# Reordering the opening of an attention-then-mixer kernel: one load queue, half rows, and a first tile that gets its gain in the product

## The chip, the cores and the metric

The kernel runs on one core of one Trainium2 chip. A core has engines with instruction streams of their own: TensorE (PE, matmuls; PEld is its loading of the stationary operand), VectorE (DVE), ScalarE (ACT), GpSimd (POOL) and SyncE (SP, which here only issues loads and stores). They wait for each other by semaphores. Sixteen DMA engines move data between the device memory and the on-chip memory (SBUF, 128 partitions); PE writes its results to PSUM, in banks of 128 x 512 float32.

The metric is the device time of one execution in microseconds, as the median of several executions. The profile is taken from one more execution; its times are counted from the first instruction (the span).

## The reference

Eight batches of 576 tokens, eight heads of 64. Weights of the second block are float64 in memory.

```python
kv  = einsum('bhsd,bhse->bhde', k, v)            # 64 x 64 per head, over 576 tokens
o   = einsum('bhsd,bhde->bhse', q, kv)
rms = sqrt(mean(o * o, axis=-1, keepdims=True) + 1e-6)     # per token and head
x   = (o / rms * g_norm)                          # then heads side by side: 8 x 576 x 512
h   = relu(x^T @ w_tok1) @ w_tok2                 # over tokens: 576 -> 256 -> 576
u   = x + h^T
out = u + relu(u @ w_ch1) @ w_ch2                 # over channels: 512 -> 1536 -> 512
```

## The kernel before

**Batches and tiles.** Batches are handled in pairs. A batch's 576 rows are 512 rows, which lie in SBUF as four rows per partition (`k_in`, `v_in`, index 0 to 3 of the second axis), and 64 remainder rows (index 4, `J`). In before, a remainder is loaded as two loads of 32 rows into partitions 0 to 63 and partitions 64 to 127 of index 4 are set to zero, so that it can be multiplied like the rest. q comes transposed: `qT` with 512 tokens, `qR` with the 64 others.

**Steps of the attention** (function `attention`, lines 363 to 535). A step has a short name: `kv<s><h>` makes the product of k and v for batch s of the pair and half h of the heads, 20 matmuls of 64 x 64 per pair of head columns, 40 records in the profile, since a float32 matmul leaves two; `e<s><h>` copies it to SBUF (`kvp`); `a<c><t>` multiplies the q of one 128-token tile with it (c = 0, 1 are batch 0, c = 2, 3 batch 1, c = 4 the remainders of both). Of each tile the profile shows `g` (gain: multiply by g out of PSUM into x, DVE, L453), `q` (square, ACT, L457), `t` (sum per head, DVE, L474), `m` (mean, L479), `r` (square root, ACT, L484), `i` (four small DVE instructions, L488 to L493), and the scaling of x by the inverse: `d` on DVE (L511), `s` as eight instructions on ACT (L507), or `p` on POOL. One set of statistics (`m`, `r`, `i`) serves the two tiles of a c, 16 columns wide; for c = 4 it is 8 wide.

**Steps of the token mixing** (`token_mixing`, from line 538): `h<s><t><j>` is one matmul of 128 x 512 per token tile j of batch s and half t of the 256 hidden columns, summed over tiles in PSUM; `hr` adds the remainder; then ReLU on ACT (L130); `u<i>` multiplies by `w_tok2`.

**Weights.** float64 weights are loaded as raw words and turned to float32 by two ACT instructions (L166, L169) and three DVE ones (clamp L181, shift L185, add L190). A block's step names are `w<n>0` to `w<n>4`: the load, the two ACT instructions together, clamp, shift, add. w01 to w04 is the first 256 rows of `w_tok1`, w1x the next 256, w2x its remainder, w3x and w4x are `w_tok2`.

**Order.** `keep` (line 121) holds every engine to the order in which the program writes its instructions. The loads are written first, in the order that lines 1276 to 1284 give. Each load on SP or ACT takes one of eight semaphores in turn, so it waits at issue for the landing of the one eight before it, and everything behind it on that queue waits too. Then `play(start, ...)` (line 1349) writes the steps of the lists in lines 1304 to 1310 in reading order:

```python
"j12 kv00 e00", "kv01 gs e01 l0", "a00 g00 q00", "a01 g01 q01 t00 t01 m0 w01",
"a10 w02 r0 i0 w03 d00 w04 q10 w30 w40 lq0", "a11 q11 s01 g10 g11 w11 j8",
"h000 h010 w12 w13 w14 t10 t11 m1 r1", "kv10 e10", "kv11 e11 i1 d10 d11 l1", "h001", "a20 q20", "h011",
```

`j<n>` are n matmuls of the identity with itself whose result nobody reads; `gs` spreads g over the partitions by a matmul with a row of ones and a copy; `l0`, `lq0`, `lr0` issue the loads of the next pair. `middle`, `steady` and `last` follow with later pairs, and after them the channel mixing, which makes most of the kernel.

In before the first batch's k is loaded through SP's queue, its v and g through ACT's queue, all else through SP's. Loads stand in this order: k and v of batch 0 with remainders, q of batch 0, both blocks of `w_tok1` (256 rows each), k and v of batch 1, q of batch 1, the remainders of q, the remainder of `w_tok1`.

Of the kernel before, what the change touches and what calls it, by code (L numbers as in the profile page):

```python
# [20 lines left out]
def kernel(  # L21
# [77 lines left out]
    ident = inp.tile([P, P], F32, name="ident")  # L99
    g_sb = inp.tile([P, 1, D], F32, name="g_sb")  # L100
    g_row, ones = (inp.tile([1, n], F32, name=name) for n, name in ((D, "g_row"), (P, "ones")))
# [38 lines left out]

    def load(b):

        if b >= B:
            return

        queues = (nc.sync, nc.sync if b else nc.scalar)
        for dst, t, e in zip((k_in[b % 2], v_in[b % 2]), (k, v), queues):
            dma(dst[:, :J], t[b, :LO].rearrange("(p j) e -> p j e", j=J), e)
            for n in range(0, HF, Q):
                dma(dst[n:n + Q, J], t[b, LO + n:LO + n + Q].rearrange("(r e) d -> e r d", e=8), e)  # L150
# [11 lines left out]
    def decode(dst, raw, flat, leaves=False):  # L162

        bits = dst.bitcast(U32)
        def scale():
            keep(nc.scalar.activation(dst, raw()[..., 1].bitcast(F32), AF.Prelu,  # L166
                                      scale=2.0 ** -112, alpha=2.0 ** 32))
            low = raw()[..., 0]
            keep(nc.scalar.activation(low, low, AF.Copy, scale=2.0 ** -29))  # L169

        def scale_leaves():
            of = raw().rearrange("p (g b l j) w -> p g l b j w", g=4, b=NC, l=2)
            to = lambda t, l: t.rearrange("p (g l b j) -> p g l b j", g=4, l=2, b=NC)[:, :, l]
            for l in range(2):
                keep(nc.scalar.activation(to(dst, l), of[:, :, l, ..., 1].bitcast(F32), AF.Prelu,
                                          scale=2.0 ** -112, alpha=2.0 ** 32))
            for l in range(2):
                keep(nc.scalar.activation(to(raw()[..., 1], l), of[:, :, l, ..., 0], AF.Copy, scale=2.0 ** -29))

        def clamp():  # L180
            keep(nc.vector.tensor_scalar(out=dst, in0=dst, scalar1=TOP, scalar2=-TOP * 2.0 ** 32,  # L181
                                         op0=ALU.min, op1=ALU.max))

        def shift():
            keep(nc.vector.tensor_scalar(out=bits, in0=bits, scalar1=3, scalar2=None,  # L185
                                         op0=ALU.logical_shift_left))

        def add():
            o = bits.bitcast(U16)
            keep(nc.vector._custom_dve(ADD32_U16LIMBS, out=o, in0=o, in1=flat().bitcast(U16)[..., 2 * leaves:][..., :2]))  # L190

        return scale_leaves if leaves else scale, clamp, shift, add
# [23 lines left out]
    def get_tok1(i):  # L216

        rows = words(moe_w_tok1)[:LO].rearrange("(i j p) n w -> i p j n w", j=2, p=P)
        return block(2 * DTOK, lambda raw: [(raw.rearrange("p (j n) w -> p j n w", j=2), rows[i])], w_tok1[i])

# [142 lines left out]
    def attention(pair, groups):  # L363
# [9 lines left out]
        def kv(side, half):  # L373
            kk, vv = k_in[side], v_in[side]
            if whole:
                o = kv_ps[side, half] = zeroed[half]
            else:
                o = kv_ps[side, half] = ps["kv"].tile([P, 2, P], F32, name="ps_kv", tag="kv")
            for i in range(2):
                for j in range(JJ):  # L380
                    for h in range(2):
                        at = ds(half * DH + i * P + h * D, D)
                        matmul(o[ds(h * D, D), i, ds(h * D if whole else 0, D)], lhsT=kk[:, j, at],
                               rhs=vv[:, j, at],
                               start=(j == 0), stop=(j == JJ - 1), skip_group_check=True)

        def evict(side, half):
            n = P if whole else D
            o, i = kvp[side][:, 2 * half:2 * half + 2, :n], kv_ps[side, half][:, :, :n]
            if whole and side == 0:  # L390
                keep(nc.vector.tensor_copy(o, i))
            else:
                copy(o, i)

        def attend_tile(c, t):
            side = c // 2
            o = ps["o"].tile([P, DM], F32, name="ps_o", tag="o")
# [63 lines left out]

        def stats_of(c):
# [6 lines left out]
        def total(c, h):  # L469
            g = group(c)  # L470
            if g not in stat:
# [23 lines left out]
        def inv_of(c, t):  # L495

            inv = stats_of(c)[2]
# [10 lines left out]

        def scale_vector(c, t):
# [8 lines left out]
        for s in range(2):  # L518
            for h in range(2):
                steps |= {f"kv{s}{h}": do(kv, s, h), f"e{s}{h}": do(evict, s, h),  # L520
                          f"l{s}": do(load, 2 * pair + 2 + s)}
            steps |= {f"lq{s}": do(load_q, 2 * pair + 2 + s), f"lr{s}": do(load_q_rest, 2 * pair + 2 + s)}
        for c in range(5):
# [7 lines left out]
            for t in range(1 if c == 4 else 2):  # L531
                steps |= {f"{n}{c}{t}": do(f, c, t) for n, f in zip("spd", (scale, scale_pool, scale_vector))}
        for g in groups:
# [710 lines left out]
    def stream(blocks):  # L1244
# [5 lines left out]
        for n in range(len(blocks)):  # L1250
            clamp, shift, add = blocks[n][2:]
# [5 lines left out]
    def play(lines, after={}, **stages):  # L1257
# [3 lines left out]
        for name in " ".join(lines).split():  # L1261
# [5 lines left out]
            else:  # L1267
# [5 lines left out]
    tok2 = [get_tok2(t) for t in range(NTOK)]  # L1273
    channel = ([get_ch1(c, f) for f in range(2) for c in range(NC)]
               + [get_ch2(f) for f in range(NF // 2)])
    load(0)
    load_q(0)
    for block in tok1[:2]:
        block[0]()
    load(1)  # L1280
    load_q(1)
    load_q_rest(0)
    load_q_rest(1)
    tok1[2][0]()
    for t in [t for pair in zip(k_in, v_in) for t in pair]:
        keep(nc.gpsimd.memset(t[HF:, J], 0.0))
    zeroed = [ps["kv"].tile([P, 2, P], F32, name="ps_kv", tag="kv") for _ in range(2)]
    for t in zeroed:
        keep(nc.vector.memset(t, 0.0))

# [3 lines left out]
    make_identity(nc, ident)  # L1294
    keep(nc.gpsimd.memset(ones, 1.0))
    dma(g_row, bass.AP(tensor=g_norm.tensor, offset=g_norm.offset, ap=[[0, 1], list(g_norm.ap[0])]), nc.scalar)

    def spread_g():

        o = ps["h"].tile([P, DM], F32, name="ps_g", tag="h")  # L1300
        matmul(o[:, :D], lhsT=ones, rhs=g_row, start=True, stop=True)
# [3 lines left out]
        "j12 kv00 e00", "kv01 gs e01 l0", "a00 g00 q00", "a01 g01 q01 t00 t01 m0 w01",  # L1305
        "a10 w02 r0 i0 w03 d00 w04 q10 w30 w40 lq0", "a11 q11 s01 g10 g11 w11 j8",
        "h000 h010 w12 w13 w14 t10 t11 m1 r1", "kv10 e10", "kv11 e11 i1 d10 d11 l1", "h001", "a20 q20", "h011",
        "a21 q21 g20 g21 t20 t21 m2", "h002 h012 r2", "a30 g30 i2 d20 q30", "a31 q31 s21 g31 t30",
        "h003 h013 t31 m3",
        "a40 q40 r3 i3 d30 s31 g40 t40 m4 r4 w21 i4 d40 lr0 lr1"]  # L1310
# [23 lines left out]
    more = {f"w{n}{k}": f for n, b in enumerate(tok1 + tok2) for k, f in enumerate(b)}  # L1334
# [6 lines left out]
    def keep_warm(n):  # L1341

        o = ps["h"].tile([P, DM], F32, name="ps_j", tag="h")
        for _ in range(n):
            matmul(o[:, :P], lhsT=ident, rhs=ident, start=True, stop=True)

    more |= {f"j{n}": do(keep_warm, n) for n in (8, 12)}
    more["gs"] = spread_g
    play(start, attention=attentions[0], mixing=mixings[0], more=more)
# [120 lines left out]
```

## Time and profile before

| | us |
|---|---|
| median of four runs | 771.93 (771.18 to 773.28) |
| the profiled execution's own time | 773.29 |
| its span in the profile | 771.5 |
| PE busy | 760.0 (99%) |
| DVE busy | 642.6 (83%) |
| ACT busy | 277.6 (36%) |
| POOL busy | 112.3 (15%) |
| DMA, mean over the span | 244 GB/s |

How to read what follows. A line of the timeline gives the start, the time from the first start to the last end, the engine, the line of the program, the operation, what it writes and reads, how many records, and in brackets how long the engine stood idle before it and what released it. A line of the chain of waits gives start, duration and what the last instruction of the program depended on at that time. A line of the windows gives, for one stretch of time, its length and each engine's busy time. Matmuls are pipelined, so a busy PE need not be at its peak rate. "Landing records" are the trace's records of the semaphore increments by which the DMA engines report that their share of a load has landed; a load that is spread over all sixteen engines has sixteen.

### The profile page before, as it was taken

To read this page: it belongs to the slowest core of one execution; us is meant where nothing else is said; L and a number is where in the kernel's file an instruction comes from. 1 tells how busy PE (TensorE), PEld (TensorE's weight loads), DVE (VectorE), ACT (ScalarE), POOL (GpSimd) and SP (SyncE) were. 2 spreads that over 40 slices of the span, in tenths; PEclk is the share of its full clock that TensorE was granted. 3 is DMA by queue.
4 is the path that set the end of the run, shared out by engine and by line. 5 is a ranking of instruction groups with operands and counts; after the bars stand their busy time and mean duration, and the time that the engine had idled before them with its cause. 6 is when DMAs were issued, how large, how long until landed. Compare 5 with 4: busy or idle time off the path is not lost.

```text
span 771.5 us, 12678 instructions
## 1 busy us (share of the span) xinstructions
PE 760.0 (99%) x4676; PEld 611.9 (79%) x4676; DVE 642.6 (83%) x945; ACT 277.6 (36%) x556; POOL 112.3 (15%) x125
## 2 busy tenths in 40 slices
PE   7899999999999999999999999999999999999998
PEld 6555554545888888888888888888888888888887
DVE  3767887897776869989978889987998996798996
ACT  3466575764210233521144242223352224325221
POOL 1002020113410000002240001042000218000204
PEclk9999999999999999999999999999999999999999
DMA  8999999499799796589898577999659879955679
GB/s 336 346 368 366 368 372 323 138 293 346 254 285 338 268 294 194 162 275 192 228 229 265 148 222 221 255 188 270 194 158 283 175 216 209 205 150 154 151 200 119
DMA packets 137677, 188.26 MB, mean 244 GB/s; under 512 B 48658, under 2 KB 95250, under 8 KB 135570
## 3 DMA queue, kind: packets, MB, share of 16 engines
q1 hardware_dynamic: 101744, 167.54, 68.8%
q0 software_dynamic: 34816, 18.36, 16.0%
q10 hardware_dynamic: 1058, 1.57, 0.6%
q8 instruction: 37, 0.61, 0.3%
q14 instruction: 22, 0.18, 0.1%
HBM read 138.28 MB, written 49.15 MB: 243 GB/s over the span
## 4 chain that ended last, share of the span: by engine, by line
PE 96%; DMA 3%; DVE 0%; issue 0%
PE ps_d L136 28%; PE ps_b L136 19%; PE ps_a L136 19%; PE ps_u L136 8%; PE ps_h L136 8%; PE ps_v L136 5%; PE ps_c L136 3%; PE ps_o L136 2%; PE ps_w L136 2%; PE ps_kv L136 2%; DMA qT<-in_q_dram 2%; DMA v_in<-in_v_dram 1%; DMA raw<-in_moe_w_tok_dram 1%; PE ps_r L136 0%; DVE xs L127 0%
## 5 line engine op out<-in xcount | busy, mean ns | idle before, releaser
L136 PE MATMUL ps_d<-ui,w 128*128 128x256 f32 x504 | 118.6, 379 | 0.0
L136 PEld LDWEIGHTS ps_d<-ui,w 128*128 128x128 f32 x504 | 95.8, 190 | 13.0
L133 ACT COPY ps_d<-ps_a 128x768 f32<-128x768 f32 (+1 forms) x56 | 32.0, 571 | 200.2 <-PE ps_a L136 197.1
L127 DVE TENSOR_TENSOR v<-v,v 128x1536 f32<-128x1536 f32 (+2 forms) x70 | 103.3, 1483 | 0.3
L136 PE MATMUL ps_b<-sv,w 128*128 128x256 f32 x324 | 78.9, 379 | 0.0
L136 PE MATMUL ps_a<-v,w 128*128 128x256 f32 x324 | 78.8, 379 | 0.0
L1206 POOL DMA_DIRECT2D out_dram<-us x24 | 26.7, 1834 | 291.9 <-ACT p L133 286.2
L136 PEld LDWEIGHTS ps_b<-sv,w 128*128 128x128 f32 x324 | 61.2, 190 | 8.9 <-issue 0.6
L136 PEld LDWEIGHTS ps_a<-v,w 128*128 128x128 f32 x324 | 61.6, 190 | 8.4
L136 PE MATMUL ps_u<-h,w_tok 128*128 128x512 f32 (+1 forms) x160 | 64.7, 599 | 0.0
L136 PE MATMUL ps_d<-v,w 128*128 128x256 f32 x258 | 62.7, 379 | 0.0
L130 ACT ACTIVATE v<-v 128x768 f32<-128x768 f32 (+1 forms) x54 | 42.6, 821 | 55.1 <-DVE v L127 52.3
L136 PE MATMUL ps_h<-x,w_tok 128*128 128x512 f32 x128 | 57.8, 600 | 0.7 <-DVE w_tok L190 0.7
L1206 POOL DMA_DIRECT2D out_dram<-r x40 | 41.3, 1928 | 102.0 <-ACT p L133 80.3
L136 PE MATMUL ps_d<-sv,w 128*128 128x256 f32 x228 | 55.4, 379 | 0.0
L136 PEld LDWEIGHTS ps_d<-v,w 128*128 128x128 f32 x258 | 48.9, 190 | 6.6
L136 PEld LDWEIGHTS ps_u<-h,w_tok 128*128 128x128 f32 (+1 forms) x160 | 25.6, 179 | 31.1 <-issue 26.7
L136 PEld LDWEIGHTS ps_d<-sv,w 128*128 128x128 f32 x228 | 43.3, 190 | 5.9
L136 PE MATMUL ps_a<-uT,w 128*128 128x256 f32 x192 | 46.7, 379 | 0.0
L136 PEld LDWEIGHTS ps_h<-x,w_tok 128*128 128x128 f32 x128 | 23.3, 190 | 27.1 <-issue 24.1
L136 PE MATMUL ps_b<-ui,w 128*128 128x256 f32 x168 | 40.8, 379 | 0.0
L136 PEld LDWEIGHTS ps_a<-uT,w 128*128 128x128 f32 x192 | 36.5, 190 | 5.0
(169 smaller groups left out, 1289.6 us busy)
## 6 DMA issues: line engine op xcount, KB each, us to landing
w<-parts SPq DMA_DIRECT2D x168, 384.0 KB
w<-parts SPq DMA_DIRECT2D x56, 192.0 KB
uT<-blocks SPq DMA_DIRECT2D x36, 256.0 KB
k_in<-in_k_dram SPq DMA_DIRECT2D x8, 1024.0 KB
qT<-in_q_dram SPq DMA_DIRECT2D x8, 1024.0 KB
out_dram<-x POOLq DMA_DIRECT2D x16, 512.0 KB, 6.8
v_in<-in_v_dram SPq DMA_DIRECT2D x7, 1024.0 KB
raw<-in_moe_w_ch_dram SPq DMA_DIRECT2D x8, 768.0 KB
```

Source lines behind the costliest of these rows:

```text
L127: keep(engine.tensor_tensor(out=o, in0=a, in1=b, op=op))
L130: keep(nc.scalar.activation(o, a, AF.Relu))
L133: keep(nc.scalar.copy(o, a))
L136: keep(nc.tensor.matmul(*a, **kw))
L1206: keep(nc.gpsimd.dma_start(to, t()[ds(b * Q, Q), at].rearrange("p n l j -> p n (l j)"), accum_op=ALU.add))
```

## The change

All of it lies in what the first pair does.

- **Loads.** k and v of batch 0 are both issued on SP. The order becomes: k and v rows of batch 0, their remainders, the first 128 rows of `w_tok1`, q of batch 0, k and v rows of batch 1, their remainders, the next 128 rows of `w_tok1`, q of batch 1, the other 256 rows of `w_tok1`, the remainders of q, the remainder of `w_tok1`. g is loaded through POOL's queue. The first 256 rows of `w_tok1` are decoded as two blocks (w0x and w5x) of 128 rows.
- **Remainders.** For batches 0 and 1 a remainder's 64 rows of 512 are loaded as 128 half rows of 256, one per partition: v's into the first half of `v_in`'s index 4, k's into the second half. `own` holds for each partition whether it has the first or the second half row (two sums over the identity), and `spread_k` (`zk<s><h>`) writes k's half rows times that column to `k_in`, so that half h has zeros in the other partitions. The zeroing of partitions 64 to 127 (`zz<s>`) moves behind the products, for the later batches. `kv0<h>` is cut into the rows (`ka`) and the remainder (`kb`).
- **First tile.** For tile 0 no gain is applied to x. `eg` multiplies kv by g (`kvg`, DVE, L425), `ag` multiplies q with it, and `dg` (L562) scales the product by the inverse out of PSUM. Tiles 0 and 1 have statistics of their own, 8 wide (`m0<h>`, `r0<h>`, `i0<h>`, L517 to L541).
- **Order and places.** Warming matmuls use `ones` (set by DVE) instead of the identity: 21 before the products, 4 behind them, none before `h000`. The second half of batch 0's `kvp` is copied by ACT, not DVE. Tile (1, 1) uses a bank of pool `h`, tiles of c = 3 banks of `kv`. Tile 1 is scaled by DVE (`d01`) and not ACT (`s01`); tile 3 by ACT (`s11`) and not DVE (`d11`). a20 to a31 follow each other.

```diff
+    def load_rem(dst, t, b):
+        if b < 2:
+            at = ds(DH if dst is k_in[b] else 0, DH)
+            dma(v_in[b][:, J, at], t[b, LO:].rearrange("r (a d) -> (r a) d", a=2))
+            return
...
-        queues = (nc.sync, nc.sync if b else nc.scalar)
-        for dst, t, e in zip((k_in[b % 2], v_in[b % 2]), (k, v), queues):
...
+        else:
+            for f in (load_rows, load_rem):
+                for dst, t in pairs:
+                    f(dst, t, b)
...
+        def evict_gain(half):
+            if not half:
+                sq["kvg"] = work.tile([P, H, D], F32, name="kvg", tag="sq", bufs=3)
+            keep(nc.vector.tensor_mul(sq["kvg"][:, 4 * half:4 * half + 4],
+                                      kv_ps[0, half].rearrange("p i (h d) -> p (i h) d", d=D),
+                                      g_sb.to_broadcast([P, 4, D])))
+
+        def attend_gain():
+            o = ps["h"].tile([P, DM], F32, name="ps_og", tag="h")
+            bank["g"] = o
+            for hp in range(HP):
+                matmul(o[:, ts(hp, P)], lhsT=qT[0][:, hp, ts(0, P)], rhs=sq["kvg"][:, 2 * hp:2 * hp + 2], start=True, stop=True)
...
+        def scale_first():
...
+            keep(nc.vector.tensor_mul(of(X[pair, 0][:, 0]), of(bank["g"]), inv_of(0, 0).to_broadcast([P, HP, 2, D])))
...
+    dma(g_row, bass.AP(tensor=g_norm.tensor, offset=g_norm.offset, ap=[[0, 1], list(g_norm.ap[0])]), nc.gpsimd)
     load(0)
+    first_rows[0][0]()
     load_q(0)
-    for block in tok1[:2]:
-        block[0]()
     load(1)
+    first_rows[1][0]()
     load_q(1)
+    tok1[1][0]()
...
+    own = stats.tile([P, 2], F32, name="own")
+    keep(nc.vector.tensor_reduce(own, ident.rearrange("p (r a) -> p a r", a=2), axis=AX.X, op=ALU.add))
+
+    def spread_k(side, half):
+        o, i = (t[side][:, J, ds(n * DH, DH)] for t, n in ((k_in, half), (v_in, 1)))
+        if side == half == 0:
+            keep(nc.vector.tensor_scalar(out=o, in0=i, scalar1=own[:, :1], scalar2=None, op0=ALU.mult))
+        else:
+            keep(nc.scalar.activation(o, i, AF.Copy, scale=own[:, half:half + 1]))
...
     start = [
-        "j12 kv00 e00", "kv01 gs e01 l0", "a00 g00 q00", "a01 g01 q01 t00 t01 m0 w01",
-        "a10 w02 r0 i0 w03 d00 w04 q10 w30 w40 lq0", "a11 q11 s01 g10 g11 w11 j8",
-        "h000 h010 w12 w13 w14 t10 t11 m1 r1", "kv10 e10", "kv11 e11 i1 d10 d11 l1", "h001", "a20 q20", "h011",
-        "a21 q21 g20 g21 t20 t21 m2", "h002 h012 r2", "a30 g30 i2 d20 q30", "a31 q31 s21 g31 t30",
-        "h003 h013 t31 m3",
-        "a40 q40 r3 i3 d30 s31 g40 t40 m4 r4 w21 i4 d40 lr0 lr1"]
+        "j21 zk00 zk01 ka00 ka01 gs kb00 e00 kb01 e01 zz0 eg0 eg1 l0 w01 w02 w03 w04 j4",
+        "a00 q00 t00 m00 r00 i00", "a01 q01", "ag dg g01 t01 m01", "a10 q10", "a11 q11 r01 zk10 zk11 i01 w51 d01 w52 w53 w54",
+        "w30 w40 lq0 h000 h010", "kv10 e10 g10", "kv11 e11 zz1 g11 t10 t11 m1 r1 i1 d10 w11 w12 w13 w14 l1", "h001", "h011", "a20 q20",
+        "a21 q21 s11", "a30 q30", "a31", "h002 h012 g20 g21 t20 t21 m2 r2 i2 d20 g30 q31 s21 g31 t30",
+        "a40", "h003 h013 t31 m3",
+        "r3 i3 d30 q40 s31 g40 t40 m4 r4 w21 i4 d40 lr0 lr1"]
...
-            matmul(o[:, :P], lhsT=ident, rhs=ident, start=True, stop=True)
+            matmul(late["junk"][:, :P], lhsT=ones, rhs=ones, start=True, stop=True)
```

## The prediction

> **What bounds the kernel now.** I read the page's shares first, then the same by stretches.
>
> ```profile
> PE 760.0 (99%) x4676; PEld 611.9 (79%) x4676; DVE 642.6 (83%) x945; ACT 277.6 (36%) x556; POOL 112.3 (15%) x125
> ```
>
> ```profile
> 0.00:12.30 12.30, 8.00 (x106) 7.63 (x106) 1.24 (x5) 1.49 (x2) 2.76 (x11) 1.00 0.82 304
> 12.30:27.40 15.10, 11.73 (x135) 9.04 (x134) 11.94 (x28) 7.72 (x21) 0.00 (x0) 1.00 1.02 346
> 27.40:46.40 19.00, 18.96 (x156) 11.62 (x156) 14.51 (x37) 10.64 (x31) 0.00 (x0) 1.00 0.99 364
> 60.00:120.00 60.00, 60.00 (x803) 32.42 (x802) 51.56 (x111) 37.40 (x93) 12.13 (x16) 1.00 1.01 371
> ```
>
> Columns: stretch, PE, PEld, DVE, ACT, POOL busy, granted clock, DMA share, GB/s. From 27.4 us on PE has no gap; only the first 27.4 us can give time. Next the chain of waits, which says what set those 27.4 us:
>
> ```profile
> 0.75 7.87 DMA v_in<-in_v_dram
> 8.64 5.07 DMA raw<-in_moe_w_tok_dram
> 13.73 13.58 DMA qT<-in_q_dram
> 27.44 1.13 PE ps_o L136 x8
> ```
>
> Loads to 27.3, PE afterwards. The load that ends last is q of the second batch (q1), issued at 13.73 because its issue waits for an earlier load. The timeline shows what PE did meanwhile:
>
> ```profile
> 3.34 4.98 PE L136 MATMUL ps_j<-ident 128*128 128x128 f32 x24 [3.34 <-POOL ident masks.py:199]
> 12.34 2.05 PE L136 MATMUL ps_o<-kvp,qT 128*128 128x128 f32 x16
> 16.87 1.95 PE L136 MATMUL ps_j<-ident 128*128 128x128 f32 x16
> 19.49 1.98 PE L136 MATMUL ps_h<-x,w_tok 128*128 128x512 f32 x4 [0.68 <-DVE w_tok L190]
> 22.79 2.76 PE L136 MATMUL ps_kv<-v_in,k_in 128*64 128x64 f32 x80 [1.31 <-DMA v_in<-in_v_dram]
> ```
>
> (A float32 matmul leaves two records.) ps_j is warming work that nobody reads. From a00 at 12.34 to `hr`, at 46.39, pass 34.05 us. By the chain's prices (128-wide 0.111 a record, 512-wide 0.43, kv 0.032) the needed work in it is 64 x 0.111, 32 x 0.43, 160 x 0.032 and 1.0 for ps_r: 27.0. So 7.0 us are 1.8 of junk, waits, pipeline ends and changes of operand.
>
> **The loads.** k0 and v0 (1.05 MB each) are issued at 0.75 and the later lands at 8.62; in 14 to 19 us, with SP's queue alone, the windows give 419 GB/s. 2.10 MB at that rate are 5.0, so 2.9 us are fixed. Landing = 0.75 + 2.9 + bytes ahead / 419. The issue itself: a load waits on the queue for the one eight before it, q1 in before for raw (13.71); after, for v0's remainder, at 9.3, so it is queued 4 us sooner. Batches 0 and 1 need 8 loads instead of 12, and the eight 32-row issues of about 0.69 on SP and ACT become four of some 0.38; w_tok1 has one more.
>
> Before, q1 has 7.86 MB up to its end: 22.4. The landing records of q1 are eight engines at 21.9 to 22.8, seven at 24.0 to 25.2 and one at 27.31: remainder loads as 32 rows use eight engines only, and one engine also fetched instructions; it ran 1.5 us behind the rest at k1's landing (17.98, then 19.47), 2.1 at q1's.
>
> After, all loads stand on SP's queue in this order: k0, v0, two remainders of 0.13 on all engines, half of w_tok1 (0.26), q0, k1, v1, remainders, second half, q1. By the formula: v0 8.6; remainders 9.3; q0 (3.67 MB) 12.4 against a landing of 12.12 before; k1, v1 and remainders (6.03 MB) 18.0; second half 18.7; q1 (7.34 MB) 21.2. With a lagging engine, 1.5 to 2.1 more: 19.5, 20.2, 23.3. One queue for v0 instead of two costs an issue (0.38) hidden by k0's transfer. The half rows are 1 KB pieces, which no load of before has. Nearest rows: qR in 256-byte pieces, 18 ns a packet, and 2 KB pieces, 84 ns; eight packets an engine make a remainder 0.14 to 0.67. I take 0.3 by bytes, between the two; four of them reach from -0.7 to +1.4 us at q1, which has slack (below).
>
> **The path to a00.** Junk needs the vector memset of `ones` alone, so it starts near 1.2 instead of 3.34. Before, its records are 213 ns apart until 7.56, 4.2 us after it began, then 112. So 20 slow and 22 fast records of the 42 (j21): 6.7 us, to 7.9. Then v0 at 8.6: ka00, ka01 64 x 0.032 = 2.0; g's spread 0.4; kb00, kb01 16 records 0.5, with k's remainder already spread (DVE 0.29 by the 128x256 clamp, ACT 0.43 by the 128x256 decode, after 9.3): 11.5. Eviction 0.42, now one half on DVE and one on ACT (0.37), lies beside j4 (8 records, 0.9), which ends at 12.4. a00 at 12.5: 0.2 lost. Were no record fast (42 x 0.213), junk would end at 10.2 and a00 come 1.3 later. The new small work on DVE (memset of `ones`, two sums of the identity, each under 0.3) ends by 4.5 and waits for POOL's identity, done at 3.3 before and not more than the 0.9 of a POOL issue later now; nothing needs it before 9.3. The Trainium skill ("TensorE: Matmul & The Clock Gate", section on the HAM clock gate) says that the slow state ends after a busy window of about 3.4 us that runs free, not from the first matmul. By it the wake-up could come up to 6.8 us after 1.2, junk would end at 9.2 and a00 start 0.3 later than by the row; the result would be 0.3 us worse.
>
> **First tile.** PE gains `ag`, 8 records, 0.9. kv times g is two DVE multiplies 128x256 out of PSUM, not in the trace: between the copy 128x256 (0.42) and the gain 128x512 (0.69); 0.45, nearest the copy of equal size. They run from 11.6 to 12.5 while PE has j4 and a00 to do; uncovered, they would delay ag, 14.3, from above 1.3 each. Statistics of half a tile: a00's end 13.7, square 0.60, reduce 0.68, mean to scaling 1.33 (the 8-wide set, 40.52 to 41.85), scaling out of PSUM 0.69 (L453, L511): 17.2. The half weight on DVE (0.29 + 0.29 + 0.42) ends at 13.6. So h000 starts at 17.3, not 19.49, while a01, ag, a10, a11 (32 records, 3.6) keep PE until 17.0; j8's 1.8 and the 0.59 behind ACT's square go: the fourth tile goes to an `h` bank, and a00's bank is no longer read by a gain. ACT loses the 2.02 of s01; DVE gets 0.68 for it (d01).
>
> **Second tile row.** h000, h010 1.7 to 19.0; kv10 and kv11, 2.5, wait a little for the spread on ACT (0.43 after 19.5), to 22.1. DVE: gain 0.64, reduce 0.64, 1.33, scaling 0.68, to 20.5; second half of w_tok1 to 22.1 (ACT's 0.43 + 0.42 start at 20.6). h001, h011 1.7 to 23.9. q1, 23.3, is there: a20 to a31, 32 records, 3.6, to 27.5.
>
> **What is late next: DVE.** Its chain from 22.15, by the x2 rows: gains 1.28, reduces 1.27, 16-wide statistics 1.44 (23.54 to 24.98), scaling 0.68, w_tok1's other block 1.70 (20.61 to 22.31): h002 at 28.6. PE waits 1.1 there, which is q1's slack. Same set without the weights: x of tile 4 at 33.3, tile 6 at 38.0. PE: h002, a40, h003 4.5 to 33.1; h10 pairs 3.6 from 33.35; kv 1.3; h12 pairs 3.6; kv 1.3: tile 3's scaling, now 2.02 on ACT behind two squares, ends near 29.8, before h003 at 31.4. `hr` at 43.2; then 1.9 and a0 1.1: ps_u at 46.3. DVE ends the last weights at 41.3 + 1.1 + 1.82 + 1.82 = 46.0, just in time. Before:
>
> ```profile
> 46.34 0.76 DVE L190 CUSTOM_DVE_ANT_1 w_tok<-w_tok,raw 128x1152 uint16<-128x1152 uint16 x1
> 49.56 0.69 DVE L453 TENSOR_TENSOR x<-ps_o,g_sb 128x512 f32<-128x512 f32 x1 [2.46 <-PE ps_o L136]
> ```
>
> DVE stood still for 2.46 us there. ps_u began at 49.40, so **3.1 us are gained**, nearly all that DVE's idle time allows. Other moved work: the four memsets of remainder rows (0.52 each) go behind kv00 and kv10 on POOL, idle from 3.4 to 54.8; batch 2's kv needs them at 37, over 20 us later. No store stands behind them before 50. The later loads keep their order on SP. v2 landed at 35.42 and was used at 40.13; the loads of batches 3 to 7 land 7 to 20 us ahead of use. So 3 us bring none onto the path, the less as everything ahead of k2 leaves the queue sooner.
>
> **Sum.** The profiled execution took 773.29 (span 771.5); less 3.1, 770.2. It is 1.36 above the median of 771.93, so the median comes to 768.8. Bounds: without PE's waits in 17 to 34 us 1.5 more; with every junk record slow (1.3) and an operand change of 0.1 at some fifteen places not hidden (1.5), 2.8 less, both at once unlikely. The 1 KB pieces at their upper end bring q1 to 24.7, 0.8 behind a20, inside the 1.1.
>
> **Rivals.**
> (a) *DVE and ACT bind more*, 770.3. ACT's spread of k1 and half weight stand ahead of both kv evictions; a load at 22 instead of 20.2 moves h001, a20 and the DVE chain 1.6 later: gain 1.5. For it: DVE has no gap from 17 to 46 in my sum. Against: ACT is 56% busy there (10.64 of 19.00).
> (b) *The loads come no sooner*, 771.1: the change doesn't do what it says. q1 at 27.3 as before, a31 ends 30.9, h002 2.3 later: gain 0.8. For: DMA is full (1.02) already. Against: 0.5 MB less ahead of q1 and no load on half the engines.
> (c) *Slower*: g goes to POOL's queue and PE has its spread ahead of kb00. Price: from a landing at 11.0 on each us is lost one for one; no gain from 14.1, slower by 0.2% (1.5 us) from 15.6; with a landing at 16 it would be 773.8. For: later POOL issues take 6.8 to 8.8 us whatever their size (the page and the DMA view). Against: that makes 9.6.
>
> **How the numbers follow.** Forecast (gain 2 to 4.5) 0.62; (a) 0.16, gain 0.8 to 2; (b) 0.14, gain 0 to 1.6; (c) 0.08. 0.2%, 1.54 us, is what a measurement can tell from none. (a) lies over it in two thirds, (b) hardly: faster 0.74, same 0.18, slower 0.08. Range: forecast and (a), most of (b): 767.3 to 771.3; the forecast's own is 767.4 to 769.9.
>
> **What would show it.** Right: ps_j from 1.2; a00 near 12.5; h000 near 17.3; q1 landing by 23.5; the first h of w_tok1's second block near 28.6 after a short wait for DVE L211; ps_u near 46.3; the same work later, 3 us earlier. Wrong: ps_g waiting for g_row; ps_o of batch 1 waiting for qT beyond 25; a gap at ps_u behind L211; a granted clock under 1.00.

## The result and the profile after

The changed kernel takes 770.48 us (median of 41 executions, 770.17 to 771.57) against 771.54 for the kernel before beside it (62 executions, 770.52 to 773.46): a ratio of 0.9984, 95% interval 0.998 to 0.9989. That is 1.06 us, 0.14%: the interval leaves out 1, so the gain is real, but by the bound of 0.2% set in the prediction it counts as no difference, the case that had a chance of 0.18. The time lies inside the range, 1.7 above the predicted 768.8. The profiled execution took 770.47 (span 768.6), 2.8 less than the profiled one of before (773.29).

The windows of the changed kernel (stretch, PE, PEld, DVE, ACT, POOL busy, granted clock, DMA share, GB/s):

```profile
12.30:27.40 15.10, 14.78 (x162) 12.09 (x160) 12.43 (x34) 8.34 (x23) 1.23 (x3) 1.00 1.05 362
27.40:46.40 19.00, 18.60 (x195) 9.94 (x196) 16.16 (x39) 13.35 (x41) 0.00 (x0) 1.00 1.02 386
```

From 12.3 to 27.4 PE is busy for 14.78 of 15.10 us (before 11.73): the holes of the first stage are filled. In 27.4 to 46.4 DVE and ACT are busier than before (16.16 against 14.51, 13.35 against 10.64). PE's waits in the first 80 us, two of the five of the kernel before first, then all of the changed kernel (line, what was waited for: sum, times, longest):

```profile
PE ps_o L136 <- DMA qT<-in_q_dram: 0.8, 1, 0.8
PE ps_o L136 <- ACT sq L457: 0.6, 1, 0.6
```

```profile
PE ps_j L136 <- DVE ones L1349: 1.1, 1, 1.1
PE ps_kv L136 <- DMA v_in<-in_v_dram: 0.8, 1, 0.8
PE ps_h L136 <- DVE w_tok L211: 0.6, 1, 0.6
```

The waits for q, for ACT's square and for POOL's identity are gone. One new wait is left, 0.6 behind the decode of w_tok1's second block, in the place that the prediction gave it (1.1 at 28.6). The timeline's lines that answer to those of before:

```profile
1.07 6.40 PE L136 MATMUL ps_j<-ones 128*128 128x128 f32 x42 [1.07 <-DVE ones L1349]
12.36 2.02 PE L136 MATMUL ps_o<-kvp,qT 128*128 128x128 f32 x16
17.02 1.98 PE L136 MATMUL ps_h<-x,w_tok 128*128 128x512 f32 x4
18.93 2.60 PE L136 MATMUL ps_kv<-v_in,k_in 128*64 128x64 f32 x80
27.80 1.98 PE L136 MATMUL ps_h<-x,w_tok 128*128 128x512 f32 x4 [0.62 <-DVE w_tok L211]
42.34 1.99 PE L136 MATMUL ps_h<-x,w_tok1r 64*128 64x512 f32 x8
45.35 5.42 PE L136 MATMUL ps_u<-h,w_tok 128*128 128x512 f32 x12
```

ps_u, the first product with w_tok2, starts at 45.35; before it was 49.40, forecast 46.3. From there PE does the same work with a nearly constant lead: its last matmul ends at 763.86, before at 767.75. So 4.05 us were gained at ps_u and 3.89 at the last matmul, but only 2.8 in the time of the two profiled executions and 1.06 in the medians. The experiments are about those two differences.

The chain of waits between 8 and 28 us says what sets the stage now (start, duration, what):

```profile
8.53 11.38 DMA raw<-in_moe_w_tok_dram
19.93 0.46 ACT w_tok L181
21.15 0.42 DVE w_tok L211
21.57 1.20 DVE x L494 x2
22.77 1.20 DVE ms L522 x2
25.45 0.69 DVE x L566
27.05 0.70 DVE w_tok L211
27.80 1.98 PE ps_h L136 x4
```

The second 128 rows of w_tok1, queued behind k, v and the remainders of batch 1, land at 19.91; ACT begins their decode 0.02 later, and the chain goes on through DVE, with 0.22 of ACT's square root in it and no gap over 0.12, to the product at 27.80 (lines in between are left out). In the seven profiles of the changed kernel and of the variants that leave the work behind this landing as it is, the product starts 7.88 to 7.89 us after it (landings at 19.91 twice, 19.92, 20.01, 20.07, 20.14, 20.61). In all seven, fifteen of the sixteen DMA engines had delivered their share 1.11 to 1.58 sooner (18.63 in the changed kernel): the stage waits for one late engine. The lead over the work in front of it is small: ACT was free 0.12 before the landing, and DVE stood idle for 0.21 ahead of the decode.

### The profile page after: what moved, and what is told of

Its sections match the earlier page's. It is cut to its first block, busy times and chain, and to the rows that moved or that the text cites. A ratio compares the mean times of both kernels' runs of the same rounds, so it can differ in the third digit from the quotient of the medians.

```text
span 768.6 us, 12735 instructions
## 1 busy us (share of the span) xinstructions
PE 761.3 (99%) x4694; PEld 613.5 (80%) x4694; DVE 644.6 (84%) x956; ACT 279.5 (36%) x563; POOL 112.8 (15%) x125
## 4 chain that ended last, share of the span: by engine, by line
PE 96%; DMA 2%; DVE 1%; SPq 0%; ACT 0%; issue 0%; DVEq 0%
PE ps_d L136 28%; PE ps_b L136 19%; PE ps_a L136 19%; PE ps_u L136 8%; PE ps_h L136 8%; PE ps_v L136 5%; PE ps_c L136 3%; PE ps_w L136 2%; PE ps_kv L136 2%; PE ps_o L136 2%; DMA raw<-in_moe_w_tok_dram 1%; DMA v_in<-in_k_dram 1%; PE ps_r L136 0%; DVE x L494 0%; DVE ms L522 0%; DVE w_tok L211 0%
```

## The experiments

**The kernel before, once more.** Two explanations stood for the missing 1.8 us between profile and median: that the profiled execution of before was longer in just the stage that the change shortens, or that this stage is the same in every execution and the difference lies at the end of the kernel.

> The kernel before once more, unchanged, to see which of its executions the profile was. In the two profiles the first ps_u came at 49.40 (before) and 45.35 (after), 4.05 earlier, but the median moved by only 1.06 (771.54 to 770.48). Theory A: the profile of before, 773.29, was an execution whose first stage is 1.75 longer than usual, because the engine that lagged at q of batch 1 (27.31 against 25.17 for the next slowest) does not always lag there. Then executions spread over 770.5 to 773.5 by the first stage alone, and a profile of 771.2 to 771.6 shows its first ps_u at 47.3 to 47.9, with 767.75 less 1.7 for the last ps_d. Rival B: the first stage is the same in every execution (ps_u at 49.4 within 0.3) and the 1.75 lies in the end of the kernel, between the last ps_d and the end (3.76 in before's profile, 4.74 in after's).

No edit. Median 771.60 (10 executions); this profiled execution took 771.38, close to the median, where the first took 773.29. The timeline of this second execution of before:

```profile
21.36 2.71 PE L136 MATMUL ps_kv<-v_in,k_in 128*64 128x64 f32 x80
25.49 1.13 PE L136 MATMUL ps_o<-kvp,qT 128*128 128x128 f32 x8 [0.37 <-DMA qT<-in_q_dram]
47.45 5.42 PE L136 MATMUL ps_u<-h,w_tok 128*128 128x512 f32 x12
```

Up to 19.5 the two executions agree within 0.2. Then kv of batch 1 starts at 21.36, straight behind the products with w_tok1, instead of 22.79, because v of batch 1 lands at 21.17 and not at 22.66 (fifteen engines had delivered it by 21.16 in the first execution too), and the wait for q is 0.37 instead of 0.84 and ends 1.95 sooner (q at 25.35 instead of 27.31). ps_u comes at 47.45 instead of 49.40, and PE's last matmul at 765.81 instead of 767.75. The 1.95 us between the two executions lie wholly ahead of the product with q of batch 1: they come from the one DMA engine that ran behind the others. The end, from the last matmul on, is 3.76 in both, so the second explanation doesn't hold for the kernel before. Against this typical execution the change gains 2.10 at ps_u and 1.95 at the last matmul, and 0.91 in the time.

**The remainders as 32-row loads again.**

```diff
-        if b < 2:
-            at = ds(DH if dst is k_in[b] else 0, DH)
-            dma(v_in[b][:, J, at], t[b, LO:].rearrange("r (a d) -> (r a) d", a=2))
-            return
+    ... (the four memsets of partitions 64 to 127 back ahead of the loop; no spread zk, no zz;
         kv reads k's and v's remainder from the same columns)
```

> The changed kernel with the remainders of batches 0 and 1 loaded as 32-row loads again (zeros first, no spread of k), all else as changed. Eight engines then carry 16 packets of 2 KB each more by q of batch 1, the others none. Theory A (uneven engines, and where the lagging one falls, set the first stage of before): q lands 0.6 to 1.3 later (after 22.6, then 23.2 to 24 and more where the lagging engine is one of the eight), the second batch's kv starts 0.3 to 1 later, and the spread of the executions grows from 0.3 towards the 1 to 2 us of before; median 770.5 to 771.5. Rival B (DVE's chain to 27.8 sets the stage, the loads have slack): first ps_u within 0.2 of 45.35, median within 0.3 of 770.48, spread unchanged.

Median 770.97, 0.5 above the changed kernel. Its timeline:

```profile
13.44 2.02 PE L136 MATMUL ps_o<-kvp,qT 128*128 128x128 f32 x16 [0.71 <-DMA qT<-in_q_dram]
46.14 5.42 PE L136 MATMUL ps_u<-h,w_tok 128*128 128x512 f32 x12
```

The four 32-row loads of batch 0 land 0.31 to 0.33 after one another (from v's rows at 8.05 to 9.34), the two half-row loads 0.37 and 0.35 (from 8.14 to 8.86); q of batch 0 lands at 13.31 instead of 12.22 (fifteen engines by 12.86), and the first tile waits for it. From there the chain of waits runs through ACT and DVE to the product with the second block, at 28.59, with no load in between. ps_u is 0.79 later; the end is 0.35 shorter here (4.42), so the median shows less. So the half rows are worth 0.8 at ps_u, and they pay at q of batch 0, ahead of the first tile, not at q of batch 1.

**The first tile by the gain.**

```diff
-        "... e01 zz0 eg0 eg1 l0 w01 w02 w03 w04 j4",
-        "a00 q00 t00 m00 r00 i00", "a01 q01", "ag dg g01 t01 m01", ...
+        "... e01 zz0 l0 w01 w02 w03 w04 j4",
+        "a00 q00 g00 t00 m00 r00 i00", "a01 q01", "d00 g01 t01 m01", ...
```

> The changed kernel with its first tile through the gain as before (square, then gain, then the scaling on DVE), without kv times g and without its product. PE has 0.9 less work, DVE has a gain of 0.69 between square and sum. If DVE's chain sets the stage (the waits of the changed kernel name only w_tok's add at 27.8): scaling of tile 0 0.6 later, h000 near 17.6 instead of 17.02, first ps_u 0.3 to 0.7 later, median 770.8 to 771.2. If PE's work sets it: first ps_u 0.3 to 0.9 earlier, median 769.6 to 770.2. If neither, within 0.2 of 770.48.

Median 770.98, 0.5 above the changed kernel. The timeline:

```profile
14.96 2.05 PE L136 MATMUL ps_o<-kvp,qT 128*128 128x128 f32 x16 [0.52 <-DVE x L494]
17.61 1.98 PE L136 MATMUL ps_h<-x,w_tok 128*128 128x512 f32 x4 [0.59 <-DVE x L566]
45.65 5.42 PE L136 MATMUL ps_u<-h,w_tok 128*128 128x512 f32 x12
60.64 0.38 PE L136 MATMUL ps_r<-kvp,qR 64*64 64x64 f32 x9 [0.94 <-issue]
```

PE saves the eight records of `ag` (0.9) and loses more: 0.52 because a bank is read by a gain, 0.59 because the scaling comes later. ps_u is 0.30 later. So the product with kv times g is worth 0.3 at ps_u at most: the second block of w_tok1 landed 0.17 later in this execution (20.08), and that alone would have moved ps_u by as much. Where the rest of the 0.5 in the medians lies was not traced. (The 0.94 at 60.64 is a stop that the other profiles don't have; its cause stays open.)

**q of batch 0 ahead of the weights.**

```diff
-    first_rows[0][0]()
     load_q(0)
+    first_rows[0][0]()
```

> The changed kernel with the first half of w_tok1 loaded behind q of batch 0 instead of ahead of it: 0.26 MB, 0.6 us at 419 GB/s, leave the path of q. In the changed kernel a00 starts at 12.36, right behind q's landing at 12.22, and kv's second half is in SBUF at 11.75. Theory: a00 at 11.8 to 11.9, statistics and everything behind on DVE 0.4 to 0.5 earlier, first ps_u 44.9, median 770.0 to 770.1. Rival: the half weight, now landing at 12.2, comes into DVE's order ahead of the first sum and takes the gain back (sum not before 13.9 against 14.16): first ps_u within 0.2 of 45.35, median within 0.2 of 770.48.

Median 770.47: no difference. q lands 0.66 sooner (11.56), but the first tile starts at 12.38, because PE's four warming matmuls of `j4` end only then. No gain is the rival's number; that `j4` is the reason was in neither theory. A later run has q first and no `j4`.

**The end of the program.** From PE's last matmul to the end of the span the changed kernel takes 4.77 us, before 3.76 in both profiles. The work there is the same. DMA queue lines, from 758 us on, of the changed kernel, of which the kernel before has only one q14 and no q8:

```profile
q8 instruction: 1, 0.02, 0.4%
q14 instruction: 2, 0.02, 0.4%
```

And the waits of SP's queue from 764 us on, first the kernel before (second execution), then the changed one (line, what was waited for: sum, times, longest):

```profile
SPq L124 <- DMA out_dram<-xg: 1.7, 2, 0.9
SPq L1465 <- PEq L1465: 0.2, 1, 0.2
```

```profile
SPq L124 <- DMA out_dram<-xg: 1.6, 1, 1.6
SPq L1542 <- PEq L1542: 1.0, 2, 0.8
```

The programs are fetched in blocks by DMAs of their own, PE's in 16 KB on q8, the others' in 8 KB on q14. The traces don't name the owner, but the counts fit PE: q8 has 37 fetches in every profile with at most 9,673 traced instructions on PE and its weight loads, and 38 in every one with 9,688 or more. The changed program has 36 matmul and weight-load instructions more on PE, 7 instructions more on POOL, 2 on SP. In it a 16 KB fetch falls 1.75 us ahead of PE's end; one DMA engine delivers its share of an earlier store 0.85 behind the other fifteen (0.52 against -0.33, counted from the last matmul), the last stores of SP wait for that store's semaphore and are issued 0.59 and 1.04 after the last matmul instead of -0.74 and 0.49, and the last landing is at 3.00 instead of 2.62. Then POOL stands still for 0.35 inside the closing barrier and SP for 0.33 ahead of it. That these are block borders is suggested by their place: SP's stop lies 3, 5 and 8 instructions ahead of the end of programs that have 850 (before), 852 (changed) and 855 (32-row loads) traced ones on SP, so each time behind the 847th, and an 8 KB fetch starts 0.6 to 0.8 behind the end of each such stop. The kernel before has its stop too, but inside the barrier, where its end stays at 3.76. These runs test it: the kernel before with the changed kernel's instruction counts, and the changed kernel with other counts.

```diff
 (kernel before)
-        for _ in range(n):
-            matmul(o[:, :P], lhsT=ident, rhs=ident, start=True, stop=True)
+        for _ in range(17 if n == 8 else n):
+            w = 60 if n == 8 else P
+            matmul(o[:, :w], lhsT=ident, rhs=ident[:, :w], start=True, stop=True)
+    (7 one-column memsets on POOL, 11 on DVE, 4 one-column copies on ACT, 2 drains on SP)
```

> The kernel before, with as many instructions more on each engine in its first stage as the changed one has: the 8 warming matmuls after the first tiles as 17 of less than half the width (the same time, 36 instructions more on TensorE), 7 one-column memsets more on POOL, 2 empty instructions on SP, 9 small ones on DVE, 4 on ACT, all where these engines wait. Theory that the end of the program is longer because of where the borders of the engines' code blocks fall (a block is fetched by a DMA, and an engine at a border waits): from the last matmul to the end 4.4 to 4.8 us and not 3.76, a 16 KB fetch within 3 us ahead of the last matmul, and a median 0.7 to 1.0 above the kernel before. Rival, that the end is longer because of the order in which the changed program's stores and semaphores come: 3.76 as before, and no difference in the median.

Median 773.84 (5 executions) against 771.41 beside it. The end grows from 3.76 to 5.02, and the fetch is there, 1.63 ahead of PE's end; two of SP's waits:

```profile
SPq L124 <- DMA out_dram<-xg: 3.1, 2, 1.7
SPq L1475 <- PEq L1475: 1.0, 2, 0.8
```

Instructions alone, placed 740 us earlier, make the end of the kernel before like that of the changed one. The direction is as expected, the size larger, and the median is 2.4 above and not 0.7 to 1.0: besides 1.26 at the end the profiled execution (773.52) lost 0.57 by ps_u, where the 34 narrow warming records took 3.90 and not the 1.95 of the 16 full ones that they replace, and 0.28 later, which was not traced.

```diff
 (changed kernel)
+    for _ in range(6):
+        keep(nc.gpsimd.memset(pad[0], 0.0))
+    for _ in range(8):
+        keep(nc.sync.drain())
```

> The changed kernel with 6 one-column memsets more on POOL and 8 empty instructions more on SP in the first stage, where both wait. By the theory of the code borders POOL's border moves ahead of the closing barrier (there it cost 0.35) and SP's to where SP waits for the last stores (0.33): from the last matmul to the end 4.0 to 4.2 instead of 4.77, median 0.5 to 0.7 below the changed kernel's 770.47, so 769.8 to 770.0. TensorE's fetch 1.75 ahead of its end stays, and with it the wait of the last store but one. By the rival 4.77 and 770.5.

Median 769.83 (11 executions, 769.59 to 770.77), as expected; 0.9983 of the kernel before, interval 0.9974 to 0.9992. PE's last matmul ends at 763.83, as in the changed kernel; from the last landing to the end pass 1.05 instead of 1.77; the last landing, with the fetch still there, comes at 3.29. Fourteen instructions that do nothing make the changed kernel 0.5 to 0.6 us faster: 0.65 by the two medians, which were not measured side by side, and 0.52 by their leads over the kernel before measured beside each (1.06 and 1.58).

```diff
-        "... l0 w01 w02 w03 w04 j4",
+        "... l0 w01 w02 w03 w04",
```

> The changed kernel without the four warming matmuls ahead of the first attention tile (16 instructions fewer on TensorE). By the theory of the code borders TensorE's last fetch falls so close to its end, or behind it, that no store is late: the last stores are issued within 0.5 of the last matmul (before 0.59 and 1.04), from the last matmul to the end 4.3 to 4.5, median 770.0 to 770.2. The first stage keeps its length (q of batch 0 lands at 12.2 and the first attention tile starts there): first product with w_tok2 at 45.2 to 45.4. By the rival 4.77 and 770.5.

Median 770.66: the expected 770.0 to 770.2 missed. The mechanism is right: no 16 KB fetch, the last stores issued at -0.40 and 0.49, the last landing at 2.66. But SP's and POOL's borders remain (1.95 from landing to end), and the profiled execution started later: k and v of batch 0 land 0.46 and 0.37 later than in the changed kernel, by two or three late engines, PE's warming ended late too, and everything behind follows (ps_u 46.05).

The ends side by side (us after PE's last matmul, from the sequencers' records and DMA packets of the traces):

| kernel | 16 KB fetch | last SP store | last landing | landing to end | end |
|---|---|---|---|---|---|
| before, both profiles | none | 0.49 | 2.62, 2.63 | 1.14, 1.13 | 3.76 |
| changed | -1.75 | 1.04 | 3.00 | 1.77 | 4.77 |
| before with the counts | -1.63 | 1.16 | 3.00 | 2.02 | 5.02 |
| changed with 14 pads | -1.16 | 1.53 | 3.29 | 1.05 | 4.34 |
| changed without j4 | none | 0.49 | 2.66 | 1.95 | 4.61 |
| q first, no j4, pads | none | 0.49 | 3.00 | 1.24 | 4.24 |
| 17 warming, pads | none | 0.49 | 3.00 | 1.24 | 4.24 |

The late store follows the fetch in all fourteen profiles: in the seven with a 16 KB fetch in the last 2.1 us ahead of the last matmul, SP's last store is issued 2.69 to 2.79 after the fetch, at 0.72 to 1.53; in the seven without one it is issued at 0.49.

**q first, without j4, with the pads.** The edits are those of the three kernels above.

> The changed kernel with q of batch 0 ahead of w_tok1's first half, without the four warming matmuls, and with the pads of the kernel with 6 memsets and 8 empty instructions. Theory: q lands at 11.5, so without the four matmuls the first attention tile starts behind the evictions at 11.8 to 11.9 instead of 12.36, and the end is as short as before, 3.7 to 4.0. If DVE's chain follows the first tile, the first product with w_tok2 comes 0.3 to 0.5 sooner, at 44.9 to 45.1, and the median is 769.0 to 769.3. Rival: the loads of batch 1 (v at 18.5, its remainder at 19.2) set the rest of the stage, so the half us is lost before the second batch's kv: 45.3 as in the changed kernel, median 769.4 to 769.7.

Median 769.98. The first tile starts where it was expected, but the gain is gone by the second half of w_tok1:

```profile
11.74 2.02 PE L136 MATMUL ps_o<-kvp,qT 128*128 128x128 f32 x16 [0.38 <-DVE kvp L418]
16.73 1.98 PE L136 MATMUL ps_h<-x,w_tok 128*128 128x512 f32 x4 [0.28 <-DVE x L562]
27.90 1.98 PE L136 MATMUL ps_h<-x,w_tok 128*128 128x512 f32 x4 [0.61 <-DVE w_tok L211]
```

0.62 sooner at the first tile, 0.29 at the first h, 0.10 later at 27.90: that weight block landed at 20.01, and 7.89 later its chain ends. The rival is right for the stage: loads, not PE, set it. Its median (769.4 to 769.7) is missed as well, since the end is 4.24, not 3.7 to 4.0.

**The changed kernel again, and fewer warming matmuls.**

> The changed kernel once more, beside the next two on the same chip: 770.3 to 770.7, first product with w_tok2 at 45.3 to 45.5, from the last matmul to the end 4.7 to 4.8.

770.53 (11 executions), ps_u at 45.35, end 4.82: as expected, but for 0.02 at the end.

```diff
 (changed kernel with the 14 pads)
-        "j21 zk00 ...
+        "j17 zk00 ...
```

> The changed kernel with 6 memsets more on POOL and 8 empty instructions more on SP, and 17 warming matmuls instead of 21 ahead of the first product (16 instructions fewer on TensorE). By the theory of the code borders all three borders have left the end: no 16 KB fetch within 3 us ahead of the last matmul, last stores within 0.5 behind it, from the last matmul to the end 3.8 to 4.2; the warming still reaches its fast records (17 take 6.0 instead of 6.4 us), so the first stage is as long, 45.3 to 45.5; median 769.4 to 769.7, under the changed kernel by 0.8 to 1.0. Rival: fewer warming matmuls leave TensorE slow at the first kv: 64 records longer than 2.08, the first stage up to 1 us longer, median 770 or more.

Median 770.28, a miss of 0.6. The fetch is gone and the stores are on time, but the end is 4.24: the pads moved the 8 KB fetches to 1.04 and 2.26 after PE's end, among the last stores, and the last landing is 3.00 all the same. kv of batch 0 takes 2.08, as before: 17 warming matmuls were enough in this execution. But k of batch 0 again had late engines (two, at 5.97, the others by 5.60), kv starts 0.37 later and ps_u is at 45.58. Whether this later start belongs to the program or to the execution stays open. Of all kernels run, the changed one with the 14 pads alone has the lowest median.

**The order of the loads.**

```diff
     load(0)
-    first_rows[0][0]()
     load_q(0)
-    load(1)
-    first_rows[1][0]()
-    load_q(1)
-    tok1[1][0]()
+    first_rows[0][0]()
+    first_rows[1][0]()
+    tok1[1][0]()
+    load(1)
+    load_q(1)
```

> The changed kernel with its loads in the order of before (q of batch 0, the three blocks of w_tok1, k and v of batch 1, q of batch 1), on the same queue. 0.79 MB of weights come ahead of v of batch 1 and 0.52 MB more ahead of q of batch 1; at 419 GB/s that is 1.9 and 1.3: v at 20.3, its remainder at 21.1, q at 23.9. If the order of the loads makes a part of the gain, kv of batch 1 starts at 20.4 instead of 18.93, and with the 0.6 of slack ahead of the second block of w_tok1 the first product with w_tok2 comes 0.8 to 1.4 later, 46.2 to 46.8, median 0.8 to 1.4 above the changed kernel. Rival, that the gain is all in the work of DVE, ACT and TensorE and the loads are hidden: 45.4 and the same median.

Median 772.32, against 770.53 for the changed kernel measured beside it and 771.49 for the kernel before. The timeline:

```profile
20.84 2.89 PE L136 MATMUL ps_kv<-v_in,k_in 128*64 128x64 f32 x80 [1.74 <-DMA v_in<-in_v_dram]
47.31 5.42 PE L136 MATMUL ps_u<-h,w_tok 128*128 128x512 f32 x12
```

v of batch 1 lands at 20.70, 2.2 later, and ps_u comes 1.96 later: more than expected. With the old order of the loads all the rest of the change gains 0.14 at ps_u (47.31 against 47.45, one execution each). The kernel is slower than before for two reasons: the end is 0.60 longer than the 3.76 of before, and 0.5 lie outside the profiled span, where the time exceeds the span by 2.16 to 2.35 in all eleven executions, against 1.74 to 1.86 in the kernel before beside it; what that is was not found. Its POOL program is one instruction shorter, and POOL's stop of 0.35 in the barrier is absent (end 4.36): the border again.

**One move of the order of the loads alone.**

```diff
 (kernel before)
     load_q(0)
-    for block in tok1[:2]:
-        block[0]()
+    tok1[0][0]()
     load(1)
     load_q(1)
+    tok1[1][0]()
 (its decode w11 to w14 moves behind d11)
```

> The kernel before, with only one thing of the change's order of loads: the second block of w_tok1 (0.52 MB) is loaded behind q of batch 1 instead of ahead of k and v of batch 1, and its decode stands behind the scaling of tiles 2 and 3 instead of ahead of them. Theory that the loads set the first stage only where the work ahead of them has been shortened: in the kernel before, kv of batch 1 starts at 21.36 straight behind the products with w_tok1, and TensorE waits only 0.37 for q of batch 1, so the gain is 0.4 at most, first product with w_tok2 at 47.0 to 47.9 (47.45 in the kernel before without a lagging DMA engine), the median 771.2 to 771.9; what it brings more goes to executions with a lagging engine, so their spread narrows. Rival, that the order of the loads is most of the gain by itself: 45.4 to 46.0 and a median of 769.6 to 770.2.

Median 771.50 against 771.64, interval of the ratio 0.9989 to 1.0006: no gain, as the theory said. The block now lands at 26.39, the product with it waits 1.40 for its decode, and ps_u is at 48.21 in this execution. The spread did not narrow (770.66 to 773.10), so that part of the expectation is wrong. As far as these two runs go, this move of the order gains nothing alone, and the change without its order gains 0.14; the whole change gains 2.1. The full new order without the rest was not run.

## Why the prediction was right or wrong

**The stage: the mechanism right, the gain 0.95 too small.** The forecast took the path through a00 (12.5, measured 12.36), h000 (17.3; 17.02), the product with the second block (28.6; 27.80) and `hr` (43.2; 42.34) to ps_u (46.3; 45.35). "What is late next: DVE" is what the chain shows. Of the 0.95, 0.8 lie in the term "Its chain from 22.15, by the x2 rows": it begins at 21.57, since the half block's decode stands on ACT from 19.93, not 20.6, and two gains and two sums take 1.20 per pair where the sum has 1.28 and 1.27, since they overlap by 0.08. What the forecast did not see is how exact the balance is: it took q of batch 1 as the load with slack and DVE as the bound, but DVE's chain begins with a load, the second half of w_tok1, at 19.91. Its rival (a) had a price for just this, a load 1.8 later for 1.6 us; with v of batch 1 landing 2.2 later ps_u came 1.96 later. Small sums in the prediction are off: the first tile's terms add up to 17.0, not 17.2 (measured 17.02), and a warming that ends at 9.2 or 10.2 would by its own terms bring a00 0.5 or 1.5 later, not 0.3 or 1.3; no warming ended after 8.78.

**The loads: right, with the late engine.** q of batch 0 12.4 (12.22), second half 18.7, or 20.2 with a late engine (19.91), q of batch 1 21.2 or 23.3 (22.62); remainders 0.3 each (0.35 to 0.37). One engine was late again: k of batch 1 has fifteen engines by 14.70 and the last at 15.98. A 16 KB instruction fetch starts at 13.04; that it is the cause is suggested by the end of the kernel and was not tested here.

**The failed step: "it is 1.36 above the median, so the median comes to 768.8".** It takes the excess of the profiled execution as spread evenly, or as lying where the change does nothing. The second profile of before shows that the excess, 1.95, was in the very stage that the change shortens, so subtracting both counts it twice. The sum against the profile itself, 770.2, is 0.3 from the 770.47 measured, but that is luck: 0.95 more gained at ps_u and 1.01 lost at the end nearly cancel. That the time lies inside the range is owed to the same luck and to a range that was drawn to hold the rivals. A typical execution of before has ps_u at 47.45, and from it the forecast stage would have gained 1.15, the real one 2.10. The median of 771.93 that the forecast was counted from stood on four executions; 62 give 771.54.

**The term that was missing: +1.0 at the end.** The sum held every instruction of the first stage, and none of the work after 50 us changed. But longer programs moved borders of the instruction blocks to places in the last 7 us where they cost time: 0.37 by the late store and 0.64 by two stops, 1.01 of the 1.95 gained at PE's last matmul. "The same work later, 3 us earlier" held for PE to its last record and not for the end of the kernel.

**The rivals.** (a) DVE and ACT do bind, but the late load of its price of 1.6 did not come. (b) is refuted for the changed kernel: q of batch 1 lands at 22.62 and PE does not wait for it. (c) g landed on POOL's queue at 7.5, ahead of PE's first product at 8.27, and PE did not wait for it. Of the four signs of error none appeared: the granted clock is 1.00, q of batch 1 is in time, ps_u starts without a gap, ps_g doesn't wait. All four looked at the first 50 us; the loss came at 764.

## What to carry to other kernels

Before a profiled execution's excess over the median is taken off a forecast, find the place of the excess, with a second profile if there is one: if it lies in what the change removes, it is already in the gain. Loads and compute that were both near their limit gave next to nothing one by one here (0 and 0.14 of 2.1), so a change to either is to be judged by what the other does at that place. And a change that adds instructions to an engine's program moves the block borders in it: here one microsecond was lost at the end of the kernel, in code that nobody touched, and fourteen idle instructions gave half of it back.

## What the runs showed of the hardware

- **Instruction fetches cost time at the end.** The Trainium skill ("Runtime: NRT & Kernel Launch", section on instruction fetch mechanics) says that programs stream in 16 KiB blocks and that a crossing is mostly hidden. For PE the size agrees (16,384 bytes on q8); the fetches of the other engines here are 8,192 bytes (q14). In the changed kernel PE's list of waits has none behind 27.80, with 36 of the 38 fetches on q8 still to come, so there they are hidden. Behind the last matmul they are not: POOL stood still for 0.35 to 0.38 ahead of its last instruction in all six profiles whose POOL program has the changed kernel's length, and for 0.06 in those with 1, 6 or 7 instructions fewer or 6 more.
- **The warming time varies.** From the first warming matmul to the first fast record (112 ns a record instead of 213) pass 2.9 to 5.9 us in thirteen profiles (3.1 in the changed kernel's first, 4.4 in both of before); in the fourteenth no record is fast before the warming ends, 5.3 us after it began. The prediction used the one row, 4.2; the Trainium skill's rule that it set beside it ("TensorE: Matmul & The Clock Gate", section on the HAM clock gate: a window of about 3.4 us that runs free), read as the prediction read it (up to 6.8), covers the longest of these, but 2.9 lies below its window. Where it came late (5.9), the warming ended at 8.78 and kv of batch 0 began 0.2 behind v's landing.
- **The spread of executions.** The middle half of the executions lies within 0.22 us in the changed kernel and 1.2 in the kernel before (771.17 to 772.34). The late engine explains the one pair of profiles; what narrows the spread was not found, since neither the 32-row loads (770.89 to 771.22) nor the old order of the loads (772.22 to 772.48) widens it again in the changed kernel, and the moved block doesn't narrow it in the kernel before.
